# Four unread matrix products in front of the transposes of chunks 2 to 6

## The chip, the cores and the metric

The kernel runs on one core of one Trainium2 chip. The metric is the device time of one execution in microseconds (us); the figure given for a kernel is the median of its runs. A profile is of one execution of its own. "PE" is the matrix engine (TensorE), "DVE" is VectorE, "ACT" is ScalarE, "POOL" is GpSimd, and "SP" is SyncE, which here only issues transfers (DMAs).

## The reference

Two parts follow each other. The first is a gated linear attention over 4 batches, 8 heads, 768 steps and a head size of 48; the second is a feed-forward block on its output, taken as 3072 tokens of 384 values.

```python
# part 1, for each batch and head
for t in range(768):
    state = alpha[t, :, None] * state + outer(k[t], v[t])    # 48 x 48
    y[t] = q[t] @ state
# part 2; x is y with the heads side by side, 3072 x 384
a, b = x @ w1, x @ w2          # 384 x 1024 each
out = ((a * b) @ w3) @ w_out   # 1024 x 1024, 1024 x 384
```

The weights arrive as 8-byte floats, q, k, v and alpha as float32; the output is float32.

## The kernel before, in words

**Part 1** cuts the sequence into chunks of 128 steps: 6 chunks for each of 4 batches, 24 in all, numbered n = 0 to 23. A chunk passes through these helpers, each named in the code:

- `logs(n)` takes the logarithm of alpha on ACT (L272). `decays(n)` sums it along the chunk by a product on PE (L287) and takes the exponentials of the sum with both signs on ACT (L293, L294), the tile `e`.
- `decayed(n)` multiplies k and q by `e` on DVE (L303), which gives the tile `qk`. It needs the transfers of k and q (`load_kq`, L138 and L139) and both exponentials.
- `transposed(n)` turns q and k round on PE, 16 small transposes of 64 by 64 into two banks of PSUM (L325), and ACT copies both banks to the tile `qkT` (L327).
- `scores(n)` forms q times k on PE (L365, 8 products) and masks it on DVE (L368, two halves), the tile `ms`. `attend_state(n)` (L385) and `attend(n)` (L391) form the output of the chunk on PE, and ACT copies it to the tile `x` (L395), from which SP stores it in the scratch array `xd` (L262).
- `outer(n)` updates the state: a product on PE (L337) that DVE adds (L345, L347).

**The weights** arrive as 8-byte floats and are turned into float32 by DVE and ACT in the steps of `to_fp32` and `load_gates`. For one piece these are, in this order: the transfer `raw` (L192), ACT's `rest` (L200), DVE's `mant` and `power` (L201, L204), ACT's `power` (L205), then DVE's L207, L208 and L210, ACT's L217 and DVE's L219. `third` (L233, L234) forms a third part of a piece on PE, which ACT copies (L235).

**Part 2** works on groups of 3 chunks (384 tokens). `load_x` fetches a group from `xd` (L407, the tile `xT`), and `split_x` splits it in three parts: L413 on ACT, then L414 and L415 on DVE. The gate products are all at L421, in products of three such parts by three parts of a weight. From there on the kernel is a long row of such products: gates first, then the fold of w3 with w_out (its transposes are at L523), then the projection.

**The order.** The main loop runs over n and calls the helpers for several chunks in each turn: for turn n it calls `attend_state(n - 1)`, `scores(n)`, `transposed(n + 1)`, `attend(n - 1)`, `outer(n)`, `decayed(n + 2)`, `decays(n + 3)` and `logs(n + 4)`. Steps of the weight conversion (`convert`) lie between them in the turns up to `FIRST - 1` = 5, and the first group's `split_x` is called at the end of turn 5. The order of these calls is not the order on the engines. The language's scheduler takes the whole program, estimates how long each instruction takes and when its inputs are there, and places instructions on each engine's queue accordingly; `after_marks` tells it to place some after others. It also hands out the 8 banks of PSUM, all of one pool (`bank()`), and adds the semaphore waits. Each engine then works through its own queue in that fixed order. SP issues the loads and the stores in one queue, and some of v's loads go through POOL's.

Of the kernel before, what the change touches and what calls it, by code (L numbers as in the profile page):

```python
# [48 lines left out]
def kernel(  # L49
# [12 lines left out]
    nc = tc.nc  # L62
    B, H, S, D = q.shape
    C = 128
# [4 lines left out]
    NP = H // 2  # L69
# [6 lines left out]
    CW = 512  # L76
    AHEAD = 4
    LATE = 10
    assert D <= DP and DM % C == 0 and DF % CW == 0 and S % C == 0 and N % G == 0
    assert DM <= 512 and TG <= 512  # L80

# [21 lines left out]
    def bank():  # L103
        return ps.tile([C, 512], FP32, tag="bank", name="bank")
# [3 lines left out]
    def after_marks(*names):  # L108
        stack = ExitStack()
        for x in names:  # L110
            stack.enter_context(tc.issue_after(mark[x]))
        return stack
# [21 lines left out]
    def load_kq(n):  # L134
        if n >= N:
            return
        st["kq", n] = inp.tile([C, 2, H, D], FP32, tag="kq", name="kq")
        nc.sync.dma_start(out=st["kq", n][:, 0], in_=rows(k, n))  # L138
        nc.sync.dma_start(out=st["kq", n][:, 1], in_=rows(q, n))  # L139

    def load_v(n):
        if n < N:
            st["v", n] = vs[n % len(vs)]
            (nc.gpsimd if 2 < n < 8 else nc.sync).dma_start(out=st["v", n][:, :, 0:D], in_=rows(v, n))
# [10 lines left out]
    ident = const.tile([C, C], FP32, name="ident")  # L155
# [81 lines left out]
    def fetch(ahead=3):  # L237
        while weights and len(begun) < ahead:
            begun.append(weights.popleft())
            next(begun[-1])  # L240
# [17 lines left out]
    def store():  # L258

        while later:  # L260
            dst, src = later.popleft()
            nc.sync.dma_start(out=dst, in_=src)  # L262

    def last(n):
        return n % NCH == NCH - 1

    def logs(n):
# [4 lines left out]
        nc.scalar.activation(la, a, AF.Ln)  # L272
        if n >= LATE:

# [6 lines left out]
    def decays(n):  # L281
# [3 lines left out]
        la = st.pop(("la", n))  # L285
        if n < LATE:
            nc.tensor.matmul(lc, sums[:, n % 2].bitcast(FP32), la, start=True, stop=True)  # L287
# [26 lines left out]
    def transposed(n):  # L314
        if n >= N:
            return
        qk = qks[n % 3]
        qkT = work.tile([C, 2, NP, C], FP32, tag="qkT", name="qkT")

        tp = [bank().rearrange("p (i j c) -> p i j c", i=2, j=NP) for _ in range(2)]  # L320
        for i in range(2):
            for j in range(NP):
                for half in range(2):
                    s = ds(DP * half, DP)
                    nc.tensor.transpose(tp[half][:, i, j, :], qk[s, i, 2 * j:2 * j + 2, :], ident[s, s])  # L325
        for half in range(2):
            mark["qkT", n] = nc.scalar.copy(qkT[:, :, :, ds(DP * half, DP)], tp[half]).ins  # L327
        st["qkT", n] = qkT

    def outer(n):  # L330
        if n >= N or last(n):
            return
        qk, vc = qks[n % 3], st["v", n]
        s1 = bank()[:, 0:NP * D].rearrange("p (j d) -> p j d", j=NP)
        for j in range(NP):
            for i in range(2):
                nc.tensor.matmul(s1[ds(DP * i, DP), j, :], qk[:, 0, 2 * j + i, :], vc[:, 2 * j + i, 0:D],  # L337
                                 start=True, stop=True)

        if n % 2:  # L340
            to = st["T", n] = work.tile([C, NP, D], FP32, tag="tmp", name="tmp")
        else:
            to = Ts[1][:, :, 0:D]
        if n % NCH == 0:
            nc.vector.tensor_copy(out=to, in_=s1)  # L345
        else:
            nc.vector.tensor_add(to, s1, Ts[n % 2][:, :, 0:D])  # L347
# [233 lines left out]
    decays(0)  # L581
    decayed(0)
    transposed(0)
    with after_marks(("e", 0)):
        logs(1)
# [7 lines left out]
    load_a(4)  # L593


    FIRST = 6
    begin = {FIRST - 3 + 4 * g: (g, range(FH if g < 4 else KF)) for g in range(5)}
    loads = {8: 1, 11: 2, 15: 3, 19: 4}

    for n in range(N + 1):  # L600
# [4 lines left out]
        raws = (3, 3, 3, 3, 2, 2, 3, 3)[n] if n < 8 else 4  # L605
        for m in (n + 3,) * (n <= FIRST) + (n + 4,) * (n >= FIRST):
            load_kq(m)
            if n < FIRST - 2:
                fetch(raws)
            if n >= FIRST:  # L610
                load_v(m - 1)
        if n:
            attend_state(n - 1)
        if n < N:
            scores(n)
        transposed(n + 1)
        if n < FIRST:
            with after_marks("pool"):
                load_v(n + 2)
        if n - 2 in begin and n > FIRST:  # L620
            g, tiles = begin[n - 2]
# [142 lines left out]
```

## Time and profile before

| what | value |
| --- | --- |
| time, median of 3 runs | 477.14 us (476.88 to 477.63) |
| the profiled execution: its own time | 476.57 us |
| the profiled execution: span from first to last instruction | 474.8 us |
| mean granted clock of TensorE | 0.989 of full |
| PE busy | 456.5 us, 96% of the span |
| weight loads busy | 432.7 us, 91% |
| DVE busy | 359.1 us, 76% |
| ACT busy | 279.6 us, 59% |
| POOL busy | 76.6 us, 16% |

Times inside the profile are counted from the start of the span. Busy time is the time in which an engine works on an instruction; the ends of matmuls are modelled, and matmuls overlap, so a busy PE is not PE at its peak. "L303" is line 303 of the kernel before. A row such as "qk<-kq,e" names the tile that is written and the tiles that are read. In brackets at the end of a row of a timeline stands how long the engine was idle ahead of it, and what ended that. Idle time matters only on an engine that others wait for.

### The profile page before, as it was taken

To read this page: it belongs to the slowest core of one execution; us is meant where nothing else is said; L and a number is where in the kernel's file an instruction comes from. 1 tells how busy PE (TensorE), PEld (TensorE's weight loads), DVE (VectorE), ACT (ScalarE), POOL (GpSimd) and SP (SyncE) were. 2 spreads that over 40 slices of the span, in tenths; PEclk is the share of its full clock that TensorE was granted. 3 is DMA by queue.
4 is the path that set the end of the run, shared out by engine and by line. 5 is a ranking of instruction groups with operands and counts; after the bars stand their busy time and mean duration, and the time that the engine had idled before them with its cause. 6 is when DMAs were issued, how large, how long until landed. Compare 5 with 4: busy or idle time off the path is not lost.

```text
span 474.8 us, 10017 instructions
## 1 busy us (share of the span) xinstructions
PE 456.5 (96%) x3836; PEld 432.7 (91%) x3836; DVE 359.1 (76%) x578; ACT 279.6 (59%) x555; POOL 76.6 (16%) x144
## 2 busy tenths in 40 slices
PE   4878899999999999999999999999999999999997
PEld 2666689899999998999999999999999999999996
DVE  2778796899979888999999868855542876666761
ACT  4668765768668563988877675654543533333330
POOL 3433122104201310121221202111011000000000
PEclk9988899999999999999999999999999999999999
DMA  9999999999899944467685532202012976555511
GB/s 179 216 209 189 228 187 247 221 239 224 184 221 206 240 142 136 137 207 251 204 271 164 182 128 84 99 35 101 33 51 88 257 233 191 163 166 174 177 51 50
DMA packets 148783, 80.29 MB, mean 169 GB/s; under 512 B 99360, under 2 KB 140576, under 8 KB 148736
## 3 DMA queue, kind: packets, MB, share of 16 engines
q1 hardware_dynamic: 142960, 64.44, 55.5%
q0 software_dynamic: 5776, 15.22, 10.2%
q8 instruction: 30, 0.49, 0.5%
q14 instruction: 17, 0.14, 0.1%
HBM read 57.58 MB, written 22.06 MB: 168 GB/s over the span
## 4 chain that ended last, share of the span: by engine, by line
PE 85%; DMA 5%; DVE 4%; ACT 2%; issue 1%; SPq 1%; POOL 1%; DVEq 0%; ACTq 0%; POOLq 0%
PE bank L421 70%; PE bank L365 4%; DMA kq<-in_q_dram 4%; PE bank L391 3%; PE bank L325 2%; PE bank L385 2%; PE bank L523 1%; PE bank L337 1%; PE bank L287 1%; DMA xT<-xd 1%; PE bank L290 1%; DVE qk L303 1%; DVE ms L368 1%; DVE x L415 1%; SPq L262 1%
## 5 line engine op out<-in xcount | busy, mean ns | idle before, releaser
L421 PE MATMUL bank<-x,w 128*128 128x384 f32 x1152 | 212.6, 338 | 1.1 <-DVE x L415 0.6
L421 PEld LDWEIGHTS bank<-x,w 128*128 128x128 f32 x1152 | 200.2, 188 | 4.0 <-PE bank L421 0.9
L421 PE MATMUL bank<-w3o,ab 128*128 128x384 f32 x576 | 100.2, 336 | 0.0
L421 PEld LDWEIGHTS bank<-w3o,ab 128*128 128x128 f32 x576 | 99.9, 188 | 0.0
L446 ACT ACTIVATE bank<-bank 128x384 f32<-128x384 f32 x96 | 45.7, 476 | 41.2 <-PE bank L421 40.6
L430 ACT ACTIVATE t<-bank 128x384 f32<-128x384 f32 x64 | 31.5, 494 | 57.4 <-PE bank L421 56.2
L496 POOL DMA_DIRECT2D abd<-ab x45 | 26.3, 583 | 144.9 <-DVE ab L482 126.2
L482 DVE TENSOR_TENSOR ab<-bank,r 128x384 f32<-128x384 f32 x44 | 24.4, 554 | 24.9 <-ACT bank L446 15.9
L552 DVE TENSOR_TENSOR ab<-abl,ab 128x1024 fp32r<-128x1024 f32 x24 | 29.4, 1224 | 12.3 <-ACT ab L551 12.3
L327 ACT COPY qkT<-bank 128x512 f32<-128x512 f32 x48 | 25.8, 590 | 20.5 <-PE bank L325 20.5
L551 ACT ACTIVATE ab<-abl 128x1024 fp32r<-128x1024 f32 x24 | 25.4, 1060 | 20.2 <-PE bank L421 18.3
L421 PE MATMUL bank<-wo,w3T 128*128 128x384 f32 x192 | 35.9, 334 | 0.0
L303 DVE TENSOR_TENSOR qk<-kq,e 128x768 f32<-128x768 f32 x24 | 22.9, 954 | 14.9 <-ACT e L294 8.3
L421 PEld LDWEIGHTS bank<-wo,w3T 128*128 128x128 f32 x192 | 33.5, 188 | 0.0
L368 DVE TENSOR_TENSOR ms<-bank,keep 128x512 int32<-128x512 int32 x48 | 31.2, 683 | 0.1
L432 DVE SCALAR_TENSOR_TENSOR o<-bank,t 128x384 f32<-128x384 f32 x24 | 13.4, 557 | 23.0 <-issue 13.7
L432 DVE SCALAR_TENSOR_TENSOR r<-bank,t 128x384 f32<-128x384 f32 x40 | 22.1, 554 | 11.4 <-ACT t L430 8.5
L205 ACT ACTIVATE power<-power,rebias 128x512 uint32<-128x512 uint32 (+1 forms) x36 | 25.1, 699 | 9.2 <-DVE power L204 9.0
L365 PEld LDWEIGHTS bank<-qkT 48*128 48x128 f32 x384 | 24.4, 193 | 6.3 <-issue 3.0
L365 PE MATMUL bank<-qkT 48*128 48x128 f32 x384 | 29.3, 291 | 0.4 <-ACT x L395 0.4
L553 DVE SCALAR_TENSOR_TENSOR ab<-ab,abl 128x1024 fp32r<-128x1024 f32 x24 | 29.2, 1218 | 0.0
L391 PE MATMUL bank<-ms,v 128*64 128x128 f32 x384 | 27.6, 289 | 0.0
(81 smaller groups left out, 578.9 us busy)
## 6 DMA issues: line engine op xcount, KB each, us to landing
raw<-in_moe_w_dram SPq DMA_DIRECT2D x28, 512.0 KB, 5.2
abl<-abd SPq DMA_DIRECT2D x24, 512.0 KB, 4.4
abd<-ab POOLq DMA_DIRECT2D x45, 192.0 KB, 2.8
xT<-xd POOLq DMA_DIRECT2D x9, 576.0 KB, 4.5
ac<-in_alpha_dram SPq DMA_DIRECT2D x24, 192.0 KB, 5.2
kq<-in_k_dram SPq DMA_DIRECT2D x24, 192.0 KB, 5.7
kq<-in_q_dram SPq DMA_DIRECT2D x24, 192.0 KB, 5.7
xd<-x SPq DMA_DIRECT2D x48, 96.0 KB, 4.0
```

Source lines behind the costliest of these rows:

```text
L303: mark["qk", n] = nc.vector.tensor_mul(qks[n % 3][:, :, :, 0:D], st.pop(("kq", n)), st.pop(("e", n)).rearrange("p i (h d) -> p i h d", h=H ...
L327: mark["qkT", n] = nc.scalar.copy(qkT[:, :, :, ds(DP * half, DP)], tp[half]).ins
L365: nc.tensor.matmul(sc[i][:, j, :], qkT[r, 0, j, :], qkT[r, 1, j, :], start=True, stop=True)
L368: masked = nc.vector.tensor_tensor(ms[:, i].bitcast(I32), sc[i].bitcast(I32), keep_bc, op=ALU.bitwise_and)
L391: nc.tensor.matmul(to, vc[:, 2 * j + i, :], ms[:, i, j, :], start=(n % NCH == 0 and j % HP == 0), stop=(j % HP == HP - 1), skip_group_chec ...
L421: nc.tensor.matmul(p, w[part][i], x[part][i], start=start and part == parts[0] and i == 0, stop=stop and part == parts[-1] and i == n - 1, ...
L430: nc.scalar.activation(t, p1, AF.Copy, scale=(1.0 + 1.0 / P) * scale)
L432: nc.vector.scalar_tensor_tensor(to, p2, scale, t, op0=ALU.mult, op1=ALU.add)
L446: nc.scalar.activation(p, p, AF.Copy, scale=1.0 + 1.0 / P)
L496: (nc.gpsimd if late else nc.sync).dma_start(out=abd[g][:, f, :], in_=ab)
L552: nc.vector.tensor_sub(t[:, 1], ab, t[:, 0].bitcast(FP32))
L553: nc.vector.scalar_tensor_tensor(t[:, 2], t[:, 0].bitcast(FP32), -1.0 - 1.0 / P, ab, op0=ALU.mult, op1=ALU.add)
```

## The change

`transposed(n)` allocates its two banks and then, for chunks 2 to 6, issues four products of the identity matrix by itself into the first 128 columns of the first bank, ahead of the 16 transposes. Each is a plain float32 product of 128 by 128 with 128 columns. Nothing reads the result: the transposes write over it. The constant `FIRST` is now defined at the top, with the same value. No other instruction is added or taken away in the source.

```diff
+    FIRST = 6
...
+    def unread(to, x, count):
+
+        for _ in range(count):
+            nc.tensor.matmul(to, x[0], x[1], start=True, stop=True, skip_group_check=True)
+
+    ones = ident, ident
+
...
-        tp = [bank().rearrange("p (i j c) -> p i j c", i=2, j=NP) for _ in range(2)]
+        tp = [bank() for _ in range(2)]
+        if 1 < n <= FIRST:
+            unread(tp[0][:, 0:C], ones, 4)
+        tp = [x.rearrange("p (i j c) -> p i j c", i=2, j=NP) for x in tp]
...
-    FIRST = 6
     begin = {FIRST - 3 + 4 * g: (g, range(FH if g < 4 else KF)) for g in range(5)}
```

## The prediction

> **What bounds the kernel now.** I read the page's slices first, then the busy time by stretch, then the chain of waits around the first 60 us.
>
> ```profile
> PE   4878899999999999999999999999999999999997
> PEclk9988899999999999999999999999999999999999
> DMA  9999999999899944467685532202012976555511
> ```
>
> The slices are 11.9 us each. TensorE is full from slice 6 on; the five before it have gaps and, in slices 3 to 5, a lower clock. DMA is full in just those slices. By stretch (columns: stretch, its length, busy us of PE, weight load, DVE, ACT, POOL, then clock, DMA share, GB/s):
>
> ```profile
> 52.20:60.40 8.20, 6.34 (x89) 4.75 (x88) 6.69 (x9) 6.58 (x14) 2.26 (x4) 1.00 0.93 226
> 60.40:160.00 99.60, 99.25 (x1250) 91.56 (x1251) 87.51 (x149) 67.61 (x153) 19.80 (x37) 1.00 1.01 217
> ```
>
> From 60.4 us PE idles 0.35 us in 100. So the kernel is a front that ends at 60.45 us, when the gate products (L421) start to run without a gap, and a dense rest of 414 us with nothing to absorb a delay. **Whatever moves the start of the dense part moves the end.** The question is what sets 60.45; the chain of waits there tells it (start, us, what):
>
> ```profile
> 47.43 6.22 DMA kq<-in_q_dram
> 53.65 0.02 issue
> 53.68 0.96 DVE qk L303
> ...
> 55.97 1.20 DVE ms L368 x2
> 57.16 0.60 DVE w L219
> 57.76 1.27 DVE x L414
> 59.03 1.28 DVE x L415
> 60.31 0.14 issue
> 60.45 2.34 PE bank L421 x12
> ```
>
> A transfer of q and k (chunk 7) lands at 53.65, then VectorE works without a pause until the split of x (L414, L415) lets L421 go. PE is not on this chain before 60.45. Nor is its clock: it ran at half speed from 31.7 to 38.6 and from 48.8 to 52.2, behind waits for transfers. ScalarE's part of the split, L413, waits for xT, which lands at 55.20:
>
> ```profile
> 48.74 1.05 ACT L327 COPY qkT<-bank 128x512 f32<-128x512 f32 x2
> 49.68 0.68 ACT L200 ACTIVATE rest<-raw 128x512 f32<-128x512 uint32 x1
> 50.86 0.72 ACT L205 ACTIVATE power<-power,rebias 128x512 uint32<-128x512 uint32 x1 [0.51 <-DVE power L204]
> ...
> 55.22 1.17 ACT L413 ACTIVATE x<-xT 128x1152 fp32r<-128x1152 f32 x1 [1.43 <-DMA xT<-xd]
> ```
>
> Here L413 stands behind the copies of chunk 6 and five more kinds of work, which fill 48.7 to 53.8. That is what the built order of the changed program alters.
>
> **What the Trainium skill says.** (1) "PSUM — Partial Sum Buffer", § Engine vs sequencer instructions: ScalarE's and VectorE's queues are strict FIFO, so an instruction whose input is late holds all behind it. The trace agrees: DVE idled 2.25 us (its timeline) before the multiply of chunk 7, with L208, whose inputs had been ready since about 51.6 (L205's end), next in line. (2) "TensorE: Matmul & The Clock Gate", § What's actually happening: activity is judged in windows of 3413 ns and the clock halves after an idle one. The slow stretches here are 6.8 and 3.4 us, two windows and one; but in the 6.8 us ahead of the first PE was busy for 5.13, so the trace shows a loss without an idle window. (3) Same page, § LDWEIGHTS (loading the stationary operand): columns over 1.2 GHz, 107 ns for 128 columns, used below.
>
> **The change part by part.**
>
> *The products themselves.* 5 chunks x 4 = 20 products, float32, 128x128 by 128 columns. A plain float32 product is two passes here (L365 calls 192, the page counts 384). The nearest full-array row is the float32 transposes of L523:
>
> ```profile
> 251.80 1.03 PE L523 MATMUL bank<-ident,w 128*128 128x128 f32 x8
> ```
>
> Eight passes of 0.27 each end after 1.03, so one starts every (1.03-0.27)/7 = 0.109 us, the skill's 107 ns. Four products: 8 x 0.109 = 0.87 us, twice that at half clock; all five groups 4.4 us. The gaps they can meet:
>
> ```profile
> 24.14 0.71 PE L325 MATMUL bank<-ident,qk 64*128 64x64 f32 x16 [1.12 <-DVE qk L303]
> 32.53 1.11 PE L325 MATMUL bank<-ident,qk 64*128 64x64 f32 x16 [1.19 <-DVE T L347]
> 40.70 0.66 PE L325 MATMUL bank<-ident,qk 64*128 64x64 f32 x16
> 47.71 0.71 PE L325 MATMUL bank<-ident,qk 64*128 64x64 f32 x16 [1.87 <-DVE qk L303]
> ```
>
> These are chunks 3, 4, 5, 6; chunk 2 (18.24) and chunk 5 have no gap. Nor are all gaps filled: the banks are dealt anew, and in the built program the products of chunk 3 wait for L347 (ends 23.91+0.35 = 24.26), after the multiply they should have preceded; at chunk 4 the scores now wait for L347 (32.13+0.35 = 32.48) and products and transposes follow them. PE thus falls some 1 to 3 us behind in chunks 2 to 5. Cost at the end: nothing, as long as the chain through 53.65 and 55.20, which PE does not feed, is later; a gain from a fuller clock is nothing for the same reason.
>
> *What is moved.* PE's own order is unchanged but for the products. The scheduler, which places by its own estimates, answers the longer PE work by moving others. On DVE the multiply L303 goes ahead of older work: for chunk 7 it now precedes both score masks (L368) of chunk 5 and the next weight conversion, and chunk 8's precedes the split of x. On ACT, L413 now stands ahead of the qkT copies of chunk 6, rest and power of weight piece 5, the x copies of chunk 4, a w copy (L235) and both exponentials (L293, L294) of chunk 8. SP's order is unchanged this early (it changes some 60 transfers later); POOL swaps one small transfer of ends. So xT still lands at 55.20 and chunk 7 at 53.65, and in two strict queues about 5 us of work that had been done by then now starts after them. Queued behind L413: the copies PE's scores need, and e8, which chunk 8's multiply needs.
>
> *The chain after*, with start-to-start steps from the rows of before. ACT: L413 55.22, +1.07 copies of chunk 6 56.29, +0.94 rest 57.23, +0.60 power 57.83, +0.63 x copies 58.46, +0.52 w 58.98, +0.47 exponentials 59.45, done +0.90 = 60.35. DVE: L303 53.68, masks 54.6, L201 and L204 to 56.6, then L207 waits for rest (57.91) and L208, L210 run to 59.9; L303 of chunk 8 waits for e8, 60.35; +0.88 L219 61.23; +0.60 L414 61.83; +1.27 L415 63.10, done 64.45. L421 goes at 64.6 instead of 60.45: **+4.15**. With 0.05 us for each of some six hand-overs, +4.45. I take **+4.3**. PE is ready for it: chunk 7's transposes wait for the x copies (59.0), and attend, outer, third product and six L421 need about 3.5 us, ending near 62.5.
>
> Against the profiled execution: span 474.8 + 4.3 = 479.1, plus the 1.77 us around it (476.57-474.8), 480.9. The median of the runs, 477.14, is 0.57 above that execution, so **481.4**.
>
> *Bounds of what the trace does not show.* The clock: PE will idle about 3 us between 56 and 59 us and may be at half clock from 59 on. Half speed for one window turns its 3.5 us into 5 and the first L421 into 65.6 (+1.0 more); for two windows, about +2.5. Less than +4.3 if the landings come earlier than in the trace: each us of an earlier xT takes off up to one. Another clock before 55 us: nothing either way, since ACT and DVE both sit waiting for the landings (1.43 and 2.25 us in the rows above).
>
> **Rivals.** *Clock kept, split early: faster.* If the products hold the clock and L413's earlier place pays, L414 could start at L413's end (56.39) instead of 57.68: -1.3, 475.8. For: L413 is moved forward. Against: its input lands at 55.20 whatever its place. It decides only if xT and chunk 7 land before about 50 us, when nothing behind them would wait. *Hidden anyway: no change,* 477.1: products in gaps and the order without effect. Against: the 5 us of ACT work that fill 48.7 to 53.8. *The products' own time:* were PE the bound of the front, 20 x 0.218 = 4.4 plus changes of shape gives 482.0. Against: the 4.2 us of idle PE before chunks 3, 4 and 6 and a chain without PE. *Order and clock together:* +5.3 to +6.8, 482.4 to 483.9.
>
> **How the numbers follow.** About 0.2% (0.95 us) is what a measurement can tell from none. Order alone 0.62; order with a slow clock at the start of the dense part 0.22; the products' own time 0.06; hidden 0.04; faster 0.06. Slower 0.90, same 0.04, faster 0.06. Range: 479.4 (two of the 4.3 us absorbed by earlier landings) to 484.6 (two slow windows and 0.7 us of slack).
>
> **What would show it.** Right: L413 at about 55 with the qkT copies of chunk 6 just after it; DVE idle ahead of L303 until about 53.7; the last wait of L421 for L415 ending at 64 to 65; the dense part as long as before. Wrong: L421 starting by 61, xT landing before 52, or time added after 66 us. If the groups of products were on the path, PE would have no wait between 50 and 64.

## The result, and the profile after

The changed kernel takes **482.23 us** (median of 6 runs, 480.74 to 483.04) against 477.41 us of the kernel before (6 runs, 476.88 to 478.86): a ratio of 1.0098, 95% interval 1.0080 to 1.0116, so +4.8 us where +4.3 was forecast. The profiled execution took 480.74 us with a span of 479.0, and is the fastest of the six; against the profiled execution of before it is +4.2. Times inside the profile are those of this execution. The change adds eight lines above `decays` and three more inside `transposed`, so L303 of before is now L311, L327 is L338, L413 is L424, L415 is L426 and L421 is L432; the products are L268.

The page's slices (rows: PE, TensorE's clock, DMA):

```profile
PE   4979799999999999999999999999999999999997
PEclk9988889999999999999999999999999999999999
DMA  9999999999999934466766532212012976555511
```

The slices alone hardly show where the time was added; the stretches and the timelines below place it ahead of 65 us. By stretch (length, busy us of PE, weight load, DVE, ACT, POOL, then clock, DMA share, GB/s):

```profile
52.20:60.40 8.20, 5.74 (x70) 4.67 (x68) 4.40 (x8) 4.95 (x11) 0.50 (x1) 0.81 0.98 230
60.40:65.00 4.60, 4.60 (x43) 4.29 (x40) 4.43 (x5) 3.79 (x10) 1.30 (x3) 0.60 1.00 189
65.00:164.60 99.60, 99.57 (x1255) 91.94 (x1253) 87.53 (x151) 68.70 (x155) 22.54 (x38) 1.00 1.02 215
```

Between 52.2 and 60.4 DVE worked 4.40 us where before it worked 6.69, and ACT 4.95 instead of 6.58. From 65 us PE is as dense as it was from 60.4. What ACT did in the gap (timeline; start, duration, in brackets the idle time ahead and what ended it):

```profile
50.83 0.51 ACT L280 ACTIVATE la<-ac 128x384 f32<-128x384 f32 x1
55.45 1.16 ACT L424 ACTIVATE x<-xT 128x1152 fp32r<-128x1152 f32 x1 [4.12 <-DMA xT<-xd]
56.52 1.05 ACT L338 COPY qkT<-bank 128x512 f32<-128x512 f32 x2
57.47 0.67 ACT L201 ACTIVATE rest<-raw 128x512 f32<-128x512 uint32 x1
...
60.01 0.53 ACT L302 ACTIVATE e<-bank 128x384 f32<-128x384 f32 x1
```

The split of x waits 4.12 us for xT, and the copies of chunk 6, which ran at 48.74 before, come after it at 56.52. PE's timeline holds a second story:

```profile
25.51 1.16 PE L268 MATMUL bank<-ident 128*128 128x128 f32 x8 [1.01 <-DVE tmp L358]
...
33.48 2.08 PE L376 MATMUL bank<-qkT 48*128 48x128 f32 x14 [1.67 <-DVE T L358]
35.48 2.07 PE L268 MATMUL bank<-ident 128*128 128x128 f32 x8
37.48 1.12 PE L336 MATMUL bank<-ident,qk 64*128 64x64 f32 x16
...
57.63 2.08 PE L376 MATMUL bank<-qkT 48*128 48x128 f32 x16 [2.46 <-ACT qkT L338]
```

The products of chunk 3 do not fill a wait: they wait themselves, for a bank of PSUM. Ahead of chunk 4's transposes the scores (L376, chunk 3's) wait for a bank that DVE's update of T releases; then scores, products and transposes follow one another at half clock, and the transposes of chunk 4 start at 37.48 where they started at 32.53 before. From 33.48 to 55 PE has no wait at all. Then it waits 2.46 us for the late copies. The chain of waits of this execution ends so:

```profile
51.40 5.13 DMA kq<-in_k_dram
56.53 1.05 ACT qkT L338 x2
57.59 0.04 issue
57.63 2.08 PE bank L376 x16
...
64.33 3.18 PE bank L432 x18
```

The first sum of logarithms (L295) after the start of the gate products stands at 67.35, 4.73 us later than in before (62.62); at 90.36 us before waited 0.30 us for ACT, after does not, and from 110 us to the end the rows of after that have a counterpart in before are 4.1 to 4.2 us later.

### The profile page after: what moved, and what is told of

The parts are those of the page before. It is cut to its first block, busy times and chain, and to the rows that moved or that the text cites. A ratio compares the mean times of both kernels' runs of the same rounds, so it can differ in the third digit from the quotient of the medians.

```text
span 479.0 us, 10094 instructions
## 1 busy us (share of the span) xinstructions
PE 463.1 (97%) x3876; PEld 440.4 (92%) x3876; DVE 358.9 (75%) x578; ACT 280.0 (58%) x555; POOL 78.3 (16%) x144
## 4 chain that ended last, share of the span: by engine, by line
PE 92%; DMA 4%; DVE 2%; ACT 1%; issue 1%; SPq 0%; DVEq 0%
PE bank L432 71%; PE bank L376 5%; PE bank L402 5%; PE bank L336 3%; DMA kq<-in_q_dram 2%; PE bank L396 2%; PE bank L348 2%; PE bank L534 1%; PE bank L295 1%; PE bank L298 1%; DMA kq<-in_k_dram 1%; PE bank L268 1%; DMA ac<-in_alpha_dram 1%; DVE qk L311 0%; PE bank L234 0%
## 5 line engine op out<-in xcount | busy, mean ns | idle before, releaser
L432 PE MATMUL bank<-x,w 128*128 128x384 f32 x1152 | 212.0, 338 | 0.1
L432 PEld LDWEIGHTS bank<-x,w 128*128 128x128 f32 x1152 | 200.5, 188 | 2.2 <-issue 0.5
L432 PE MATMUL bank<-w3o,ab 128*128 128x384 f32 x576 | 100.2, 336 | 0.0
L432 PEld LDWEIGHTS bank<-w3o,ab 128*128 128x128 f32 x576 | 99.9, 188 | 0.0
L338 ACT COPY qkT<-bank 128x512 f32<-128x512 f32 x48 | 25.9, 593 | 25.8 <-PE bank L336 25.8
L432 PE MATMUL bank<-wo,w3T 128*128 128x384 f32 x192 | 35.9, 334 | 0.0
L376 PEld LDWEIGHTS bank<-qkT 48*128 48x128 f32 x384 | 26.0, 204 | 10.0 <-ACT qkT L338 3.8
L376 PE MATMUL bank<-qkT 48*128 48x128 f32 x384 | 31.1, 303 | 4.1 <-ACT qkT L338 2.5
L432 PEld LDWEIGHTS bank<-wo,w3T 128*128 128x128 f32 x192 | 33.5, 188 | 0.0
L311 DVE TENSOR_TENSOR qk<-kq,e 128x768 f32<-128x768 f32 x24 | 22.9, 954 | 12.9 <-ACT e L302 8.6
```

The lines of the kernel that those rows point to most:

```text
L376: nc.tensor.matmul(sc[i][:, j, :], qkT[r, 0, j, :], qkT[r, 1, j, :], start=True, stop=True)
L432: nc.tensor.matmul(p, w[part][i], x[part][i], start=start and part == parts[0] and i == 0, stop=stop and part == parts[-1] and i == n - 1, ...
```

## The experiments

The theory at the start was that of the prediction: the place of the split of x in ACT's queue is the cost. The rivals, numbered as in the expectations, were: one, the products' own time on PE; two, the moved multiplies on DVE; three, a slow clock that the products bring on. Each experiment is compared with runs of the kernel before on the same chip; line numbers are those of after unless said otherwise. Differences in the text are of medians; the ratio is formed from the runs by itself and may differ from the quotient of the medians, by 0.8 us at most (e12). Landings differ between executions: DVE's multiply for chunk 7, where it waited for q of that chunk, started between 50.95 (e7) and 54.95 us (e5). A single profile is therefore read for the order and the waits, and for sizes only with care.

| kernel | products | median us | before us | ratio (95%) |
| --- | --- | --- | --- | --- |
| after | 20 | 482.23 | 477.41 | 1.0098 (1.0080 to 1.0116) |
| e1: split late | 20 | 481.03 | 476.72 | 1.0091 (1.0067 to 1.0115) |
| e2: order alone | 0 | 481.48 | 476.72 | 1.0098 (1.0077 to 1.0120) |
| e3: three a chunk | 15 | 478.98 | 476.72 | 1.0057 (1.0036 to 1.0078) |
| e4: eight a chunk | 40 | 486.58 | 476.72 | 1.0213 (1.0186 to 1.0241) |
| e5: split and multiplies late | 20 | 479.13 | 476.42 | 1.0054 (1.0041 to 1.0068) |
| e6: chunk 2 alone | 4 | 477.49 | 476.42 | 1.0026 (1.0011 to 1.0041) |
| e7: chunk 6 alone, eight | 8 | 477.54 | 476.42 | 1.0017 (0.9998 to 1.0036) |
| e8: chunks 4 to 6 | 12 | 478.62 | 476.42 | 1.0037 (1.0021 to 1.0053) |
| e9: e5, T first | 20 | 478.10 | 476.50 | 1.0034 (1.0021 to 1.0048) |
| e10: before, T first | 0 | 476.26 | 476.50 | 0.9988 (0.9972 to 1.0004) |
| e11: e9 with eight a chunk | 40 | 486.22 | 476.50 | 1.0197 (1.0167 to 1.0227) |
| e12: after, T first | 20 | 481.33 | 476.50 | 1.0084 (1.0054 to 1.0115) |

### e1: the split put back

```diff
-            with after_marks("l"):
+            with after_marks("l", ("e", 8)):
                 split_x(g, 0)
```

> All twenty products stay, at the same places of TensorE's order; only the first split of x (ScalarE L424) is held back behind the exponentials of chunk 8, where the kernel before has it. Theory (the place of L424 in ScalarE's order is the cost): about 478, at most 479; the products stay in the trace with their 6.4 us, and the dense part begins near 58.5 us instead of 62.5. Rival one (the products' own time on TensorE): 482, as after. Rival two (VectorE's order, which stays nearly that of after): 481 to 482. Rival three (TensorE's half clock at the start of the dense part, brought on by the products): 480 to 482, with the slow stretch still at 57 to 64 us.

Measured +4.3 us: the theory's number is missed, and on this run alone the products' own time looked right. The traces say why the split brought nothing by being moved. On DVE, then on ACT:

```profile
53.83 0.96 DVE L311 TENSOR_TENSOR qk<-kq,e 128x768 f32<-128x768 f32 x1 [1.10 <-DMA kq<-in_q_dram]
54.70 1.28 DVE L379 TENSOR_TENSOR ms<-bank,keep 128x512 int32<-128x512 int32 x2
```

```profile
56.69 0.72 ACT L206 ACTIVATE power<-power,rebias 128x512 uint32<-128x512 uint32 x1 [2.36 <-DVE power L205]
...
60.00 1.19 ACT L424 ACTIVATE x<-xT 128x1152 fp32r<-128x1152 f32 x1
```

The multiply of chunk 7 was still ahead of the masks and of L205, and waited for its landing at 53.8. ACT's `power` waited for L205, and the split stood behind it: it started at 60.00, although xT, issued at 51.1, was there 5.1 us later. One moved instruction had been put back and the other one did its work.

### e2: the order without products

```diff
+        if n == 5:
+            split_first(0, 0)          # L413 alone, ahead of transposed(6)
         transposed(n + 1)
...
+        with after_marks(*[("x1", 0)] * (n == 6)):      # copies of chunk 6
+        with after_marks(*[("x1", 0)] * (n == 4)):      # x copies of chunk 4
+        with after_marks(*[("x1", 0)] * (("x1", 0) in mark)):   # copy of w
+        with after_marks(*[("x1", 0)] * (n == 8)):      # exponentials of chunk 8
```

> The kernel before with no products at all; the first split of x and, behind it, the copies of chunk 6, rest, power, the copies of chunk 4, the copy of w and the exponentials of chunk 8 are put by hand in ScalarE's order as in after. VectorE's order differs from after in that the masks of chunk 6 and a copy of T stand ahead of the rest of the split. Theory: 481 to 484, as slow as after or a little slower, without a single product. Rival one (products' time) and rival three (clock that the products bring on): 477, as before. Rival two (VectorE's multiply by e of chunk 7 and 8 ahead): 477 to 479, since here chunk 8's stands late.

Shown are the heads of the new lines, with comments added here. Measured +4.8 us with no product in the program. In this kernel's lines (ACT's split is L417, the copies L330, the scores L368), ACT and PE:

```profile
55.47 1.16 ACT L417 ACTIVATE x<-xT 128x1152 fp32r<-128x1152 f32 x1 [6.19 <-DMA xT<-xd]
56.53 1.05 ACT L330 COPY qkT<-bank 128x512 f32<-128x512 f32 x2
```

```profile
48.16 0.72 PE L327 MATMUL bank<-ident,qk 64*128 64x64 f32 x16 [0.40 <-DVE qk L305]
...
57.64 2.08 PE L368 MATMUL bank<-qkT 48*128 48x128 f32 x16 [4.81 <-ACT qkT L330]
```

PE came to chunk 6 at 48.16, on time (47.71 before), and then stood still for 4.81 us. The split ends at 65.14, 4.84 us later than before (60.30). DVE's queue changed a little with it: the multiply of chunk 7 is one place further ahead, one mask has moved ahead of L210, and a copy of T (0.27 us to the next start) stands in front of the rest of the split. DVE's long wait there, 5.44 us, is for ACT's rest. So the order of ACT's queue, with these small shifts behind it, is **enough** for the whole loss.

### e3 and e4: three and eight products a chunk

```diff
-            unread(tp[0][:, 0:C], ones, 4)
+            unread(tp[0][:, 0:C], ones, 3)      # e3;  8 in e4
```

> Three products a chunk instead of four, fifteen in all; with three the planner leaves the first split of x behind the exponentials of chunk 8, as before. Theory: no cost to speak of, 477 to 478.5, a step between three and four. Rival one: three quarters of the loss, 481. Rival three (clock): 479 to 481 if it follows the amount of added work.

> Eight products a chunk, forty in all; the place of the first split of x in ScalarE's order is that of after. Theory: little beyond after, 482 to 485, what is beyond being products that no longer fit into waits of TensorE. Rival one: twice the loss, 487. Rival three: 482 to 486.

e3 leaves the split late and still cost 2.3 us, above the range of the theory; e4 cost 9.9, above its range too and close to rival one's 487. With 4.8 for four products the loss grows as 2.3, 4.8, 9.9: the last two are in proportion to the number of products, and e3 lies below the line (three quarters of 4.8 would be 3.6). That looks much like the products' own time. The traces show three different orders of waits. In e3 the scores wait for a bank behind a multiply which started 2.0 us later than in after (34.17 against 32.20, both waiting for q), and PE does not wait again until 61.69, within the gate products:

```profile
35.45 1.81 PE L376 MATMUL bank<-qkT 48*128 48x128 f32 x14 [3.60 <-DVE T L358]
```

In e4 PE was through with chunk 7's transposes (L336) at 60.05 and with its outer product at 61.5, and then waited 3.39 us for a piece of w, because DVE stood 4.38 us at a transfer of the weights (DVE, then PE):

```profile
61.63 0.43 DVE L202 TENSOR_SCALAR mant<-raw 128x512 uint32<-128x512 uint32 x1 [4.38 <-DMA raw<-in_moe_w_dram]
```

```profile
64.92 0.50 PE L234 MATMUL bank<-w,signs 128*128 128x512 f32 x1 [3.39 <-ACT w L218]
```

L202 of the next weight piece had been placed ahead of L208 of the piece that was wanted. Not all of e4 is order: from 42.95 us to the end of that outer product PE has no wait, and it reached chunk 7's transposes at 59.15, 4.4 us later than before. A loss that grows with the dose, the number of products, was no proof that four products a chunk cost their own time.

### e5: split and multiplies both late

```diff
-        with after_marks(*[("ms", n)] * (n < 3)):
+        with after_marks(*[("ms", n)] * (n < 3 or n == 5), *["x3"] * (n == 6)):
             decayed(n + 2)
```

on top of e1. After e1 to e4 the theory was widened: the lag of PE in the front was a second cost.

> All twenty products; the first split of x back behind the exponentials of chunk 8 on ScalarE as in e1, and now also VectorE's multiplies by e of chunks 7 and 8 put back behind the masks and behind the split. VectorE's whole order is then that of e3, and the kernel differs from e3 by five products. Revised theory (two costs side by side: the products and the banks that PSUM hands out in the front push TensorE about 2.5 us back whatever the order; the place of L424 or of the multiplies adds the rest up to the same end): 479 to 480. First theory (order alone): 477 to 478. Rival one (products' own time alone): 482.

Measured +2.7 us, in the range. Against e1 the two multiplies' place was worth 1.6 us; and e5 is not told from e3, though it has five products more. PE's lag remains, and it does not follow the number of products:

```profile
41.14 1.16 PE L376 MATMUL bank<-qkT 48*128 48x128 f32 x16 [1.16 <-DVE tmp L358]
42.24 1.16 PE L268 MATMUL bank<-ident 128*128 128x128 f32 x8
43.33 0.71 PE L336 MATMUL bank<-ident,qk 64*128 64x64 f32 x16
```

These are chunk 4's scores and chunk 5's products and transposes: q and k of chunk 5 land, DVE multiplies, then updates T and so releases a bank, and only then all three run, one after the other. In before the same scores and transposes were at 39.71 and 40.70. The clock stood at full speed in the whole of this front (1.00 from 20 to 60 us), so the lag is not the clock's. The chain of waits shows how it reaches the end without PE: from DVE's T through ACT's copies of chunk 5 (44.37) to SP's queue, which issues q of chunk 7 at 48.36 (47.43 before). It lands at 54.93, and the split ends at 62.96, 2.66 us later than before.

### e6, e7, e8: products in single chunks

```diff
-        if 1 < n <= FIRST:
+        if n == 2:                  # e6;  n == FIRST with 8 products in e7;  3 < n <= FIRST in e8
```

> Four products for chunk 2 alone, 1.1 us of TensorE. From chunk 3 on no product is left, but the planner hands out the PSUM banks as in after: the second half of the scores waits for VectorE's update of T, which stands behind a multiply by e that waits for its load; before it waited for a copy of x. The multiplies by e of chunks 5 and 6 stand earlier on VectorE, the split stays late on ScalarE. If the banks push the front: 478 to 479.5. If only the products' time counts: 477 to 477.7 (a fifth of the loss at most 1 us). If only the place of L424 counts: 476.7.

> Eight products for chunk 6 alone, 2.05 us of TensorE, put where TensorE waits 1.87 us in the kernel before (transposes of chunk 6, for the multiply by e); the banks up to chunk 5 are those of before and the split stays late. If a wait of TensorE covers what stands ahead of it: 476.7 to 477.2, with the wait gone. If the products' own time counts everywhere (eight of twenty): 478.6.

> Four products each for chunks 4, 5 and 6, twelve in all; the scores keep the banks of before (they wait for a copy of x), but the first product of chunk 4 waits for the bank that VectorE's update of T releases, where the transposes waited before; the split stays late. If the products' time beyond the waits counts: three times 1.1 us, of which the wait at chunk 6 takes up to 1.87, so about 1 to 1.5 us left, 478 to 478.5. If the banks of the scores are the cost: 476.7 to 477.3. If the products count in full: 479.6.

e6 took 477.49 us: below the range written for the banks (478 to 479.5) and in the one for the products' time alone (477 to 477.7). Its trace speaks for the banks: no product stands after chunk 2, yet PE's scores wait 2.36 and 1.92 us for DVE's T, ahead of the transposes of chunks 4 and 6, and the second of these waits is on the chain that ends in the gate products. The interval, 0.5 to 2.0 us, does not tell its four products from the banks. e8: +2.2, just above what was written for time beyond the waits; its chain passes through chunk 6's wait for T and then through its products, 2.00 us at half clock.

e7 was meant to put eight products into a wait, and did not. q of chunk 6 came early, the multiply was done at 47.1, and PE's scores ended only at 47.6. The products (1.98 us to the next start) therefore delayed the transposes, to 49.58 (47.71 before), and they stand on the chain of waits that ends in the gate products (start, us, what):

```profile
46.58 1.09 PE bank L376 x16
47.67 1.98 PE bank L268 x16
49.65 0.64 PE bank L336 x12
```

The dense part still began 0.89 us **earlier** than before's (last split wait ends at 59.56, 60.45 before), in an execution in which q of chunk 7 came earlier too: its multiply ran at 50.95 (53.68 before). And yet the span was 0.9 us longer. The early start was lost from the next split on, that of group 1, where PE waits 0.95 us and then three shorter times, 0.16 to 0.32 us; ACT, then PE:

```profile
84.71 1.17 ACT L424 ACTIVATE x<-xT 128x1152 fp32r<-128x1152 f32 x1 [1.57 <-DMA xT<-xd]
```

```profile
86.75 0.71 PE L336 MATMUL bank<-ident,qk 64*128 64x64 f32 x15 [0.95 <-ACT x L406]
```

So e7, at +1.1 us (0.3 above the range for a covered wait, interval -0.1 to +1.7), does not show whether a wait covers products. What it does show is that the same trap, a split queued ahead of copies, lies a second time at 85 us. It is in the kernel before as well: there ACT waits 0.54 us for that xT, and PE shows no wait for it.

### e9 to e12: the bank released early

```diff
-            nc.vector.tensor_add(to, s1, Ts[n % 2][:, :, 0:D])
+            mark["T", n] = nc.vector.tensor_add(to, s1, Ts[n % 2][:, :, 0:D]).ins
...
-        with after_marks(*[("ms", n)] * (n < 3 or n == 5), *["x3"] * (n == 6)):
+        with after_marks(*[("ms", n)] * (n < 3 or n == 5), *["x3"] * (n == 6), *[("T", n)] * (("T", n) in mark and n < 6)):
             decayed(n + 2)
```

The copy of T at the first chunk of a batch gets the same mark. This is e9 on e5; e10, e11 and e12 put the same `("T", n)` into the kernel before, into e5 with eight products, and into after.

> The kernel e5 (all twenty products, split and multiplies late), with one more edit: for chunks 1 to 5 VectorE's update of T is put ahead of the multiply by e two chunks on, so that the PSUM bank which the scores or the products need is released before that multiply waits for its load, and not after it. TensorE's order and the banks stay those of after. Bank theory (scores and products were pushed behind the landing by a bank that is released late, so that no wait covered them): 476.5 to 477.5, most of e5's 2.7 us returned with every product still there. Rival (the products' own time): 479, as e5.

> The control: the kernel before, no products, with the same edit as e9 (updates of T ahead of the multiplies). In the kernel before one wait of 1.19 us at chunk 4 is put down to T. Bank theory: 475.5 to 476.5, at most 0.5 us gained, as the landings pace these chunks. Rival (the edit is good for 2 us by itself, whatever the banks): 474.5.

> As e9 with eight products a chunk, forty in all, 2.05 us a chunk at full clock. The waits of TensorE in the kernel before, chunks 3 to 6, were 1.1, 1.2, 0 and 1.9 us, so about 4 us of the 10 us have no cover. If only what exceeds the waits counts and each landing starts a chunk anew: 478 to 481. If the products cost nothing: 477. If they count in full: 486.

> The changed kernel with the edit of e9 alone: the banks released early, the first split of x left at its early place on ScalarE, and the multiplies of chunks 7 and 8 at theirs. If the place of L424 by itself carries the loss, as e2 showed without products: 481 to 482. If the banks are the larger part: 478 to 479.

e9 came to +1.6 us, 1.1 less than e5, but 0.6 above what the bank theory expected. Its profiled execution (476.96) is well below its median, and shows the theory at work: with T at 35.15, ahead of the wait for the landing, chunk 4's scores and chunk 5's products run **inside** that wait, and chunks 4 to 7 reach their transposes at 32.20, 41.13, 47.43 and 53.73 (32.53, 40.70, 47.71 and 54.78 before). From 32 us on no product is on the chain of waits that leads to the gate products. DVE, then PE:

```profile
35.15 0.35 DVE L358 TENSOR_TENSOR tmp<-bank,T 128x192 f32<-128x192 f32 x1
...
40.12 0.96 DVE L311 TENSOR_TENSOR qk<-kq,e 128x768 f32<-128x768 f32 x1 [3.40 <-DMA kq<-in_q_dram]
```

```profile
36.69 1.16 PE L376 MATMUL bank<-qkT 48*128 48x128 f32 x16
37.78 1.16 PE L268 MATMUL bank<-ident 128*128 128x128 f32 x8
41.13 0.71 PE L336 MATMUL bank<-ident,qk 64*128 64x64 f32 x16 [2.19 <-DVE qk L311]
```

All twenty products are there and the span is 475.2 us, 0.4 above before's. What the other 1.2 us of the median is, no profile here shows. e10, the control, is not told from no change: the edit by itself is worth nothing that can be measured.

e12 asks whether PE's lag holds the changed kernel. PE is on time there (transposes of chunk 6 at 47.05), and the loss is still 4.8 us by the medians, 4.0 by the ratio, whose interval lies above all of e9's. ACT, DVE, then PE:

```profile
55.30 1.16 ACT L424 ACTIVATE x<-xT 128x1152 fp32r<-128x1152 f32 x1 [7.10 <-DMA xT<-xd]
```

```profile
53.77 0.96 DVE L311 TENSOR_TENSOR qk<-kq,e 128x768 f32<-128x768 f32 x1 [6.24 <-DMA kq<-in_q_dram]
```

```profile
55.39 0.80 PE L235 MATMUL bank<-w,signs 128*128 128x512 f32 x1 [6.17 <-DVE w L220]
```

ACT now waits 7.10 us for xT instead of 4.12, and DVE, which did not wait at this place in after, waits 6.24 us for q of chunk 7 at the moved multiply. PE's wait is put down to DVE's L220, which stands behind that multiply. What PE had won was waited away behind the two moved instructions, and two chains meet. The split's end at 64.54 hangs on ACT: DVE waits for its rest at 58.03 and for its exponentials at 60.44. PE comes to its gate products at 64.51, at half clock behind its wait for L220. Which of the two moved instructions is the cost here, e12 does not tell.

e11 missed its range by 5 us, and by its number, 486.22, it is the case of products that count in full (486). The trace shows two parts. PE runs without a wait from 16.79 to 59.2 us with forty products in it and reaches chunk 7's transposes at 57.04, 2.3 us later than before: that much is the products' own time. Then it stands, as in e4, because L202 of the next weight piece is ahead of L208 of the wanted one (DVE, then PE):

```profile
62.39 0.43 DVE L202 TENSOR_SCALAR mant<-raw 128x512 uint32<-128x512 uint32 x1 [6.90 <-DMA raw<-in_moe_w_dram]
```

```profile
65.67 0.80 PE L234 MATMUL bank<-w,signs 128*128 128x512 f32 x1 [6.50 <-ACT w L218]
```

The transfer that DVE waits for landed at 62.37, hardly later than in before, where ACT's work on it started at 61.65, but there nothing that the first gate products needed stood behind it. No run takes this order away, so what forty products cost by themselves stays open.

No version here beat the kernel before by more than a measurement can tell.

## Why the prediction was right, point by point

- **The bound** was read rightly. All of the added time lies ahead of the first uninterrupted gate products, the rest of the kernel is only moved, and a delay of the start reaches the end: 4.73 us at 67 us, 4.2 at the end. The 0.5 us between them were not foreseen. One reading was wrong, with nothing resting on it: DMA is full or nearly so up to slice 14, and not in just the slices of the front.
- **The moved split on ACT** is enough for the loss, as forecast: L424 at 55.45 (55.22 forecast), copies of chunk 6 right behind it. e2 gives the whole loss without products, and e12 gives it with PE on time. It is not the only instruction that can do it: with the split alone put back (e1) the moved multiply costs nearly as much, and only with both put back (e5) does 2.1 of the 4.8 us return. The Trainium skill's "PSUM — Partial Sum Buffer", § Engine vs sequencer instructions, has these queues as strict FIFO; the 7.10 us in e12, with copies ready behind the split, agree.
- **The moved multiply on DVE** was half right. In after it did not wait: q and k of chunk 7 had landed when DVE reached it at 51.77, not 53.65, and DVE idled 3.56 us later, for ACT's rest. The chain of ACT alone gave the sum. That the place can cost by itself shows between e1 and e5: 1.6 us. In e12 the multiply did wait, 6.24 us.
- **"Cost at the end: nothing, as long as the chain ... is later"** holds with its condition and only with it. In after, removing PE's lag is not told from no change (e12, 1.0084, against 1.0098), because both landings are then waited for longer. Once the split and the multiplies are back in place, the lag costs 2.7 us (e5), of which the early release returns about 1.1 (e9). The prediction had seen that the banks were dealt anew and that PE would fall 1 to 3 us behind in chunks 2 to 5; it was 4.95 at chunk 4 and 3.8 at chunk 6.
- **PE ready by 62.5** failed. PE ran at half clock from 57.2 to 64.1 (0.81 and 0.60 in the two stretches above), as one of the cases had it, was through with the last third product (L235) at 64.3 and with six gate products just after 65. The split (L426) ended at 64.67. So no wait for L426 shows, where one was forecast to end at 64 to 65, and PE was the last to be ready, by about half a microsecond. That the two chains ended so close together is luck; the +1.0 to +2.5 us priced for a slow clock did not come.
- **The products' length** was 1.09 us for a group, not 0.87: the spacing of passes was right (0.111 measured, 0.109 forecast), the 0.2 us on top of the passes, named in the prediction only as changes of shape for the rival, were left out of that sum.
- **The size**: +4.2 between the two profiled executions, +4.8 between medians; forecast +4.3. The profiled execution of after is the fastest of its runs, and what makes the others 0.7 to 2.3 us longer is not in the trace.
- **The rivals**: the products' own time would have given 482.0, nearer to the median (482.23) than the forecast of 481.4, and the losses of after and e4 are in proportion to the number of products. e2 (the loss without them) and e9 (all of them, at a third of the loss) take it away as the explanation; with four a chunk, what can be theirs is at most the loss of e9, 1.6 us (by its ratio 1.0 to 2.3). A clock slowed by the products does not explain the loss, which is there in e2 without products. Nor is the half clock at the start of the gate products needed: from 60.4 to 65 us the clock was 0.60 in after and 0.50 in e2, but 0.91 in e1, which lost 4.3.

The costs do not add: several chains, through ACT's split, DVE's multiply and PE's lag, all end at the gate products, and the latest is what the kernel pays. In the profiles the end of the split (L426 or its counterpart) goes with the loss: 60.30 in before, 62.90 in e3, 62.96 in e5, 65.06 in e1, 65.14 in e2, 69.33 in e11. Left open: the remaining 1.6 us of e9, what in e6 is bank and what is order, and what eight products a chunk cost by themselves.

## What to carry to other kernels

Where a scheduler sets the order, price what added work makes it move before pricing the work: here twenty products could be hidden down to a loss of 1.6 us, and an instruction moved ahead of a landing in a strict queue cost 4.8 us with no product in the program. Look at a wait as cover only after asking which buffer the covering work writes and who releases it; a PSUM bank released behind the very landing is no cover. A loss that grows in step with the dose is not yet a cost by dose; take the dose away and keep the order, and the other way round.

## What the runs showed of the hardware

A group of plain float32 128x128 products between operations of other shapes took 0.87 us for 6 passes (e3, 46.00 to 46.87), 1.09 for 8 (after, 44.24 to 45.33) and 1.98 for 16 (e4, 52.61 to 54.59), start to start of the next operation: 0.111 us a pass and 0.2 us a group on top. That the 0.2 us are the changes of shape is a guess; no run varies them. TensorE's clock fell to half in different places in the profiles of kernels with much the same front (mean clock from 20 to 60 us in steps of ten: 0.83, 0.79, 0.87, 1.00 in e3, and 1.00 in all of e5), and yet e3 and e5 are not told apart in time. In after it was at half from 57.2 us, though PE had idled for only 2.46 us at a stretch (55.17 to 57.63).
